# Attention into a soft mixture of experts: one pool of named places, six streams of row sums, every step's position from a table

## The chip, the cores and the metric

The kernel runs on one core of one Trainium2 chip. The metric is the device time in microseconds of one execution of the whole program; the time of the kernel before is the median of three runs. The profile is one execution taken by the hardware profiler; all times in it count from its first instruction.

## The reference, cut to what matters

Inputs are q, k, v of shape (8, 8, 576, 64), phi (512, 32), w1 (8, 512, 1024) and w2 (8, 1024, 512).

```python
q_rot, k_rot = (rotate(q), rotate(k))              # rotary positions
scores = 1/sqrt(64) * np.matmul(q_rot, k_rot.transpose(0, 1, 3, 2))
attn = np.exp(scores - np.max(scores, axis=-1, keepdims=True))
attn = attn / (np.sum(attn, axis=-1, keepdims=True) + 1e-09)
x = np.matmul(attn, v)                             # regrouped to (4608, 512)
logits = x @ phi                                   # 32 slots
d = softmax(logits, axis=0); c = softmax(logits, axis=1)
slot_input = d.T @ x                               # 4 slots for each of 8 experts
slot_out[e] = np.maximum(slot_input[e] @ w1[e], 0.0) @ w2[e]
out = c @ slot_out
```

## The kernel before, in words

**Pairs.** Two heads make a pair, so there are 32 pairs, four to a batch of the input. For each pair the queries and keys come in (`fetch`, L135), GpSimd multiplies them by cosine and sine in eight pieces (`spin`, L140), VectorE adds the halves (`join`, L144), ScalarE casts to fp16 (`high`, L149) and VectorE subtracts the cast to get the low part (`low`, L153).

**Maxima.** In nine groups of four matmuls (`m_unit`, L173, and `m_rem`, L181) TensorE makes the scores by rows into PSUM and VectorE reduces each group to row maxima (L175, L183). The maxima are turned, scaled and sent as two rows to the partitions of `peak` (`m_turn`, `m_half`, `m_rows`).

**Scores and values.** In nine blocks of keys (`t_unit`, L220) TensorE makes the transposed scores with the maximum subtracted, in 16 matmuls; ScalarE takes the exponential into `a_t` (two blocks to a tile) or `a_rem` (the ninth, L221). `av` (L236) multiplies a block with the values, four fp32 matmuls, each two records in the trace. Maxima, scores, sums, turned tiles and logits all take turns in one PSUM pool of three tiles (`bank2`).

**Row sums.** VectorE adds the four two-block tiles into `c_t` (`add`, L253 twice with 1152 columns, L255 once with 576). `total` (L265) sums the partitions of four streams (both halves of `c_t`, `a_rem`, the first half of the last `a_t`) by matmuls with a matrix of ones and zeros, eight per pair, 32 output partitions each, side by side. `total_out` (L270) copies the result out, `send` (L276) moves it by four small DMAs onto 96 partitions, `recip` (L282, L283) adds the four streams and takes the reciprocal, `spread` and `widen` bring it back over all partitions through DRAM, and `norm` on GpSimd multiplies the output of the attention.

**Slots.** From the normalised output come logits (`logits`, L348), the turned rows `xn` (`natural`, L334), and after every fourth pair the slots' running sums (`slot_tasks`, L395, L398) and the softmax over slots. After the last pair come two expert layers (`ffn1`, L773; `ffn2_steps`, L797), the collecting of slot outputs (`gather`, L810) and the output (`combine`, L825), 18 stores of 512 KB.

**Expert weights.** 64 tiles of 512 KB come through SyncE's queue (`load_w`, L482). 25 have places of their own. The others wait until a pool of the attention is closed: `release_io` after the last `low`, `release_stk` and `release_att` behind the last pair, and at last the place of `xn`.

**What sets the order.** All five engines run in the order in which the program is written. The table `WHEN` gives each step one position in a beat of four units per pair, the same for every pair; the opening and the closing are written by hand. In the opening, VectorE copies four small squares of the identity (`fold`, L630) before the first maxima.

Of the kernel before, what the change touches and what calls it, by code (L numbers as in the profile page):

```python
# [17 lines left out]
NP = H // 2  # L18
# [10 lines left out]
N_W = 25  # L29
N_WA = 5  # L30
N_WB = 2
N_WE = 3
N_WL = 2
N_X = 4
N_CS = 1
N_CE = 2
C_POOL = 4
LATE = (0, 2)
N_LEAD = 7
# [4 lines left out]
N_CST = 4 - N_CE  # L44
RC = 12
PIECE = 4
WHEN = {
    "load0": -15.9, "load1": -14.496, "spin0": -13.466, "spin1": -12.4, "join": -9.9, "high0": -9.4817, "high1":
    -9.0595, "low": -8.0, "m01": -6.5262, "m10": -5.894, "m00": -5.0601, "m11": -4.7, "load_v": -3.85, "m20": -3.771,
    "m21": -3.317, "m30": -2.9, "m31": -2.7, "m_rem": -2.6642, "m_min": -2.49, "m_turn": -1.744, "m_half": -1.667,  # L50
# [4 lines left out]
    "o_out": 4.52, "add3": 4.6009, "total": 5.54, "total_out": 5.55, "send": 5.56, "sums_turn": 6.0, "sums_wide": 6.3,  # L55
    "norm_wide": 6.4, "logits_late": 7.0, "logits_sum_late": 7.05, "recip": 7.294, "natural_late": 7.3, "spread": 7.31,
    "natural_out_late": 7.35, "widen": 7.3768, "norm": 8.706, "logits": 10.54, "logits_sum": 10.579, "stats": 11.3708,
    "natural": 11.52, "natural_out": 11.536,
}
QL, QH, KH, KL = range(4)  # L60
# [3 lines left out]
def attn_softmoe(ctx, tc, qk, v, phi, w1, w2, cs, ident, sel, seg, out):  # L64
# [5 lines left out]
    wp = ctx.enter_context(tc.tile_pool(name="wp", bufs=N_W))  # L70
    left = ctx.enter_context(ExitStack())
    xp = left.enter_context(tc.tile_pool(name="xp", bufs=1))
    vals = ctx.enter_context(ExitStack())
    late = vals.enter_context(tc.tile_pool(name="late", bufs=2))
    trans = ctx.enter_context(ExitStack())
    att = trans.enter_context(tc.tile_pool(name="att", bufs=1))
    early = ctx.enter_context(ExitStack())
    stk = early.enter_context(tc.tile_pool(name="stk", bufs=4))
    right = ctx.enter_context(ExitStack())
    io = right.enter_context(tc.tile_pool(name="io", bufs=1, side="right"))  # L80
# [5 lines left out]
        engines={mybir.EngineType.PE, mybir.EngineType.Activation, mybir.EngineType.DVE}))  # L86
    steady = ctx.enter_context(ExitStack())
    steady.enter_context(tc.manual_schedule(engines={mybir.EngineType.SP, mybir.EngineType.Pool}))

    rows = (slice(0, 64), slice(64, P))  # L90
    cs_sb = io.tile([P, 2, S], F32, name="cs_sb")
# [3 lines left out]
    bits = const.tile([P, 5], F32, name="bits")  # L95
    ones, warm, tiny, fold = bits[:, 0:1], bits[:, 1:2], bits[:, 2:3], bits[:, 3:5]
# [27 lines left out]
    c_tiles = []  # L124
# [4 lines left out]
    def load(p):  # L129
        loaded[p] = io.tile([P, 2, 2, S], F32, name="x_in", bufs=2)  # L130
# [78 lines left out]
    def t_unit(p, b):  # L209
        if b == KB - 1:  # L210
            rems[p] = att.tile([P, S], F32, name="a_rem")
        elif b % 2 == 0:
            ats[p, b // 2] = att.tile([P, 2, S], F32, name="a_t", bufs=4)
# [28 lines left out]
    def o_out(p):  # L242
        xts[p] = late.tile([P, S], F32, name="xt")
        nc.scalar.copy(out=xts[p].rearrange("p (n x) -> p n x", n=2), in_=os_.pop(p)[:, :, 0:HC])  # L244
# [13 lines left out]
    rcs = [const.tile([96, 4, RC], F32, name=f"rc{i}") for i in range(2)]  # L258

    def total(p):  # L260
        c, r, a = cts.pop(p), rems[p], ats[p, 3]
        sg[p] = s = bank2()
        for n in range(2):
            for i, m in enumerate((c[:, 0], c[:, 1], r, a[:, 0])):
                nc.tensor.matmul(s[32 * i:32 * i + 32, n, 0:HC], lhsT=pick[:, n:n + NS], rhs=m[:, half[n]],  # L265
                                 start=True, stop=True, tile_position=(0, 32 * i))

    def total_out(p):
        s, s4 = sg[p], late.tile([P, S], F32, name="s4", bufs=1)
        nc.scalar.activation(out=s4.rearrange("p (n x) -> p n x", n=2), in_=s[:, :, 0:HC], func=AF.Identity, bias=tiny)  # L270
# [15 lines left out]
    def spread(p, eng):  # L286
        rr = sg.pop(p)
        rd = dram.tile([2, S], F32, name="r_row")
        eng.dma_start(out=rd.rearrange("h (r x) -> (h r) x", x=RC), in_=rr)
        sg[p] = rd  # L290

    def widen(p, eng):
        rd = sg.pop(p)
        rbs[p] = rb = late.tile([P, S], F32, name="rb", bufs=1)
        for h in range(2):
            eng.dma_start(out=rb[rows[h]], in_=rd[h:h + 1].broadcast_to([64, S]))
# [4 lines left out]
    def sums_turn(p):  # L301
        s4 = sg.pop(p)
        t = bank2()
        for j in range(5):
            w = P if j < 4 else 64
            nc.tensor.matmul(t[0:w, 0, 2 * j:2 * j + 2], lhsT=s4[:, P * j:P * j + w], rhs=fold, start=True, stop=True)
        rn = small.tile([P, RC], F32, name="rr", bufs=2)
        nc.vector.reciprocal(out=rn[:, 0:8], in_=t[:, 0, 0:8])
        nc.vector.reciprocal(out=rn[0:64, 8:10], in_=t[0:64, 0, 8:10])
        sg[p] = rn  # L310

    def sums_wide(p):
        rn = sg.pop(p)
        sg[p] = t = bank2()
        for j in range(5):
            w = P if j < 4 else 64
            for h in range(2):
                nc.tensor.matmul(t[rows[h], j // 4, P * (j % 4):P * (j % 4) + w],
                                 lhsT=rn[0:w, 2 * j + h:2 * j + h + 1].broadcast_to([w, 64]), rhs=id_sb[0:w, 0:w],
                                 start=True, stop=True)  # L320

    def norm_wide(p):
        t, xt = sg.pop(p), xts[p]
        nc.vector.tensor_tensor(out=xt[:, 0:512], in0=t[:, 0], in1=xt[:, 0:512], op=ALU.mult)
# [609 lines left out]
```

## Time and profile before

| what | value |
|---|---|
| time, three runs | 613.80, 610.75, 618.16 us; median 613.8 |
| span of the profiled execution | 611.8 us, from the first to the last instruction; no time of its own is given beside it |
| mean granted TensorE clock | 0.959 of full speed |
| DMA | 111.63 MB in 71734 packets |
| weight loads | 63 of 512 KB under one name, one under another |

In the page, busy is the union of an engine's instructions; matmul ends are modelled. The chain of waits follows the last instruction back to what released it. Idle time of an engine costs nothing where another engine sets the end.

### The profile page before, as it was taken

How to read it: one execution, taken by the hardware profiler on the slowest of the kernel's cores; microseconds unless marked ns; L12 is line 12 of the kernel's file. 1: busy time of each engine (PE TensorE's matmuls, PEld its weight loads, DVE VectorE, ACT ScalarE, POOL GpSimd, SP SyncE). 2: the span in 40 equal slices, each digit the busy share in tenths (PEclk: the TensorE clock that was granted, in tenths of full speed). 3: DMA queues.
4: the chain of work that ended last, by engine and by line, in shares of the span. 5: the costliest groups of instructions: out<-in, count | busy, mean ns of one | idle time of the engine just before them, and what ended most of it. 6: DMA issues, size and time to landing. Idle time of an engine off the chain costs nothing.

```text
span 611.8 us, 23277 instructions
## 1 busy us (share of the span) xinstructions
PE 532.9 (87%) x10064; PEld 352.1 (58%) x10064; DVE 497.0 (81%) x729; ACT 326.9 (53%) x647; POOL 315.1 (52%) x308
## 2 busy tenths in 40 slices
PE   3668999998999899989999899898898999799981
PEld 2346666656765566666656565666566666443551
DVE  6879899999998999999998999999899874322341
ACT  2145656665665565656656566565465655324441
POOL 2668498655676566647763857658654000100000
PEclk9679999999999999999999999999899999859996
DMA  7153555555555555555555555455542246649999
GB/s 260 60 195 119 175 174 173 174 174 173 174 173 174 174 174 174 173 175 174 174 173 175 173 174 174 174 174 174 171 141 62 64 130 206 206 142 350 349 376 298
DMA packets 71734, 111.63 MB, mean 182 GB/s; under 512 B 20176, under 2 KB 47568, under 8 KB 71632
## 3 DMA queue, kind: packets, MB, share of 16 engines
q1 hardware_dynamic: 71618, 110.15, 54.5%
q8 instruction: 79, 1.29, 0.9%
q14 instruction: 23, 0.19, 0.1%
q10 hardware_dynamic: 14, 0.00, 0.0%
HBM read 99.93 MB, written 9.58 MB: 179 GB/s over the span
## 4 chain that ended last, share of the span: by engine, by line
PE 35%; DVE 26%; DMA 20%; ACT 6%; SPq 5%; issue 5%; POOL 1%; DVEq 0%; ACTq 0%
PE s_ps L220 8%; PE o_ps L236 8%; DVE nm L175 7%; DMA rc<-s 7%; DMA w_exp<-in_w 6%; DVE c_t L253 6%; DVE hl L153 5%; SPq L276 4%; ACT a_t L221 3%; PE s_ps L265 3%; DMA x_in<-in_qk 3%; PE s_ps L773 3%; DMA v_in<-in_v 2%; DVE c_t L255 2%; PE s_ps L173 2%
## 5 line engine op out<-in xcount | busy, mean ns | idle before, releaser
L140 POOL TENSOR_TENSOR x_in<-x_in,cs_sb 128x288 f32<-128x288 f32 x248 | 264.9, 1101 | 63.0 <-DMA x_in<-in_qk 38.1
L221 ACT ACTIVATE a_t<-s_ps 128x576 f32<-128x576 f32 x256 | 158.9, 649 | 97.8 <-PE s_ps L220 95.9
L175 DVE TENSOR_REDUCE nm<-s_ps 128x2 f32<-128x576 f32 x256 | 187.1, 743 | 15.1 <-PE s_ps L173 14.9
L236 PE MATMUL o_ps<-a_t,v_in 64*64 64x288 f32 x2048 | 172.4, 413 | 1.0 <-ACT xt L244 0.3
L220 PE MATMUL s_ps<-hl 64*64 64x288 f16 x3456 | 155.5, 286 | 16.4 <-DVE nm L175 15.9
L220 PEld LDWEIGHTS <-hl 64*64 64x64 f16 x3456 | 104.4, 107 | 59.9 <-issue 43.8
L299 POOL TENSOR_TENSOR xt<-xt,rb 128x576 f32<-128x576 f32 x30 | 42.8, 1425 | 141.0 <-DMA rb<-r_row 104.1
L173 PE MATMUL s_ps<-hl 64*64 64x288 f16 x1024 | 82.1, 298 | 26.0 <-DVE nm L175 20.5
L220 PE MATMUL s_ps<-peak,lift 64*64 64x288 f16 x1152 | 89.1, 284 | 0.0
L236 PEld LDWEIGHTS o_ps<-a_t,v_in 64*64 64x64 f32 x2048 | 72.9, 133 | 21.0 <-issue 7.3
L173 PEld LDWEIGHTS <-hl 64*64 64x64 f16 x1024 | 45.0, 107 | 49.1 <-issue 37.7
L149 ACT CAST hl<-x_in 128x576 f16<-128x576 f32 (+1 forms) x66 | 40.1, 650 | 33.1 <-DVE x_in L144 30.3
L270 ACT ACTIVATE s<-s_ps,bits 128x576 f32<-128x576 f32 x32 | 23.7, 740 | 58.0 <-PE s_ps L265 26.3
L144 DVE TENSOR_TENSOR x_in<-x_in 128x1152 f32<-128x1152 f32 (+2 forms) x36 | 53.4, 1483 | 0.5 <-POOL x_in L140 0.4
L253 DVE TENSOR_TENSOR c_t<-c_t,a_t 128x1152 f32<-128x1152 f32 x32 | 51.6, 1611 | 0.0
L153 DVE TENSOR_TENSOR hl<-x_in,hl 128x1152 f16<-128x1152 f32 x32 | 49.5, 1546 | 1.8 <-ACT hl L149 1.8
L253 DVE TENSOR_TENSOR c_t<-a_t 128x1152 f32<-128x1152 f32 x32 | 50.6, 1582 | 0.0
L220 PEld LDWEIGHTS <-lift 64*64 64x64 f16 x1152 | 38.1, 108 | 0.6
L265 PE MATMUL s_ps<-c_t,pick 128*32 128x288 f32 x256 | 37.1, 411 | 0.0
L265 PE MATMUL s_ps<-a_rem,pick 128*32 128x288 f32 x128 | 36.9, 411 | 0.0
L265 PE MATMUL s_ps<-a_t,pick 128*32 128x288 f32 x128 | 36.9, 411 | 0.0
L221 ACT ACTIVATE a_rem<-s_ps 128x576 f32<-128x576 f32 x32 | 20.8, 651 | 17.0 <-PE s_ps L220 17.0
(183 smaller groups left out, 597.6 us busy)
## 6 DMA issues: line engine op xcount, KB each, us to landing
x_in<-in_qk SPq DMA_DIRECT2D x62, 576.0 KB
w_exp<-in_w SPq DMA_DIRECT2D x63, 512.0 KB
v_in<-in_v SPq DMA_DIRECT2D x32, 576.0 KB
rb<-r_row SPq DMA_DIRECT2D x60, 144.0 KB
out<-w_exp SPq DMA_DIRECT2D x16, 512.0 KB
rc<-s SPq DMA_DIRECT2D x120, 4.5 KB
x_in<-in_qk SPq DMA_DIRECT2D x4, 288.0 KB
out<-w_exp SPq DMA_DIRECT2D x4, 256.0 KB
```

Source lines behind the costliest of these rows:

```text
L140: eng.tensor_tensor(out=x[:, :, c], in0=x[:, :, c], in1=cs_sb[:, :, c], op=ALU.mult)
L144: nc.vector.tensor_tensor(out=x[:, t, 0, c], in0=x[:, t, 0, c], in1=x[:, t, 1, c], op=ALU.add)
L149: nc.scalar.copy(out=halves[p][:, 1 + t, c], in_=loaded[p][:, t, 0, c])
L153: nc.vector.tensor_tensor(out=hl[:, 0:4:3], in0=x[:, :, 0], in1=hl[:, 1:3], op=ALU.subtract)
L173: nc.tensor.matmul(s[rows[c], h, 0:HC], lhsT=hl[rows[h], QH, at:at + D], rhs=hl[rows[h], KH, half[n]], start=True, stop=True)
L175: nc.vector.tensor_reduce(out=nms[p][:, n, j:8:4], in_=s[:, :, 0:HC], axis=AX.X, op=ALU.max, negate=True)
L220: nc.tensor.matmul(s[rows[h ^ n], n, 0:HC], lhsT=lhs, rhs=rhs, start=(i == 0), stop=(i == 3))
L221: nc.scalar.activation(out=weights_of(p, b).rearrange("p (n x) -> p n x", n=2), in_=s[:, :, 0:HC], func=AF.Exp, scale=SCALE)
L236: nc.tensor.matmul(o[rows[h], n, 0:HC], lhsT=vt[r, b, n], rhs=a[r, half[n]], start=(b == 0), stop=(b == KB - 1))
L253: nc.vector.tensor_tensor(out=c, in0=c if j > 1 else ats[p, 0], in1=a, op=ALU.add)
L265: nc.tensor.matmul(s[32 * i:32 * i + 32, n, 0:HC], lhsT=pick[:, n:n + NS], rhs=m[:, half[n]], start=True, stop=True, tile_position=(0, 32 ...
L299: eng.tensor_tensor(out=xts[p], in0=xts[p], in1=rbs.pop(p), op=ALU.mult)
```

## The change

One pool (`big`) holds all large tiles under fixed names, each a place: two for the inputs (`x0`, `x1`), four for the fp16 parts (`hl0` to `hl3`), two for values, four for the exponentials (`a0` to `a3`), and so on. It stays open to the end. A weight tile is loaded into a place right behind the place's last reader: `fill` is a step like the others, 0.8 units behind the last `low`, `t8` or `av8` that reads there. Weights of their own have 28 places (`w`), which also hold the later tiles of the closing part; results go out from nine of the attention's places.

The row sums have six streams, in two sets of three that accumulate in PSUM: `c` (now the sum of the first two tiles, its first half with the first half of the third added), the second half of the third, both halves of the fourth, and the ninth block. That is two additions on VectorE and twelve matmuls. The result has 288 columns, and two sends go out in place of four.

Every step has its own position for each of the four pairs of a batch, and one of its own for each of the first four pairs; the batch's steps (`ENDS`), the opening's single steps (`ONCE`) and the last pair but one (`LAST`) are in tables too. GpSimd makes `fold` in one instruction, in place of VectorE's four copies.

```diff
-N_W = 25
+N_W = 28
+LAG = 0.8
+FILL = (6, 8, 5)
+PLACES = ("x0", "x1", "cs", "hl0", "hl1", "hl2", "v0", "hl3", "a0")
-    "o_out": 4.52, "add3": 4.6009, "total": 5.54, "total_out": 5.55, "send": 5.56, "sums_turn": 6.0, "sums_wide": 6.3,
+    4.6881, 4.3287, 3.6811), "o_out": (4.8784, 4.7532, 4.6296, 4.2983), "total": (5.7529, 5.5594, 5.1412, 4.9378),
+    "total_out": (5.8475, 5.7089, 5.282, 4.971), "send": (6.4739, 6.3131, 6.1856, 5.6953), "recip": (6.8303, 6.8467,
+    7.2922, 6.5543), "spread": (7.8252, 7.2981, 7.5691, 7.5261), "widen": (8.6569, 8.8329, 7.6411, 8.2716), "norm":
...
     def add(p, j):
         if j == 1:
-            cts[p] = att.tile([P, 2, S], F32, name="c_t")
-        c, a = cts[p], ats[p, j]
-        if j < 3:
-            nc.vector.tensor_tensor(out=c, in0=c if j > 1 else ats[p, 0], in1=a, op=ALU.add)
+            cts[p] = big.tile([P, 2, S], F32, name="c")
+            nc.vector.tensor_tensor(out=cts[p], in0=ats[p, 0], in1=ats[p, 1], op=ALU.add)
         else:
-            nc.vector.tensor_tensor(out=c[:, 1], in0=c[:, 1], in1=a[:, 1], op=ALU.add)
+            c = cts[p][:, 0]
+            nc.vector.tensor_tensor(out=c, in0=c, in1=ats[p, 2][:, 0], op=ALU.add)
...
     def total(p):
-        c, r, a = cts.pop(p), rems[p], ats[p, 3]
+        c, a2, a3 = cts.pop(p), ats[p, 2], ats[p, 3]
+        streams = ((c[:, 0], c[:, 1], a2[:, 1]), (a3[:, 0], a3[:, 1], rems[p]))
         sg[p] = s = bank2()
-        for n in range(2):
-            for i, m in enumerate((c[:, 0], c[:, 1], r, a[:, 0])):
-                nc.tensor.matmul(s[32 * i:32 * i + 32, n, 0:HC], lhsT=pick[:, n:n + NS], rhs=m[:, half[n]],
-                                 start=True, stop=True, tile_position=(0, 32 * i))
+        for i in range(3):
+            for k in range(2):
+                for n in range(2):
+                    g = 32 * (n + 2 * k)
+                    nc.tensor.matmul(s[g:g + 32, 0, 0:HC], lhsT=pick[:, 16 * n:16 * n + 32], rhs=streams[k][i][:, half[n]],
+                                     start=(i == 0), stop=(i == 2), tile_position=(0, g))
...
     def send(p, eng):
         s4, rc = sg.pop(p), rcs[p % 2]
-        for i in range(4):
-            eng.dma_start(out=rc[:, i, :], in_=s4[32 * i:32 * i + 2])
+        for k in range(2):
+            eng.dma_start(out=rc[:, k, :], in_=s4[64 * k:64 * k + 64:16])
...
+    def turn_w():
+        load_w(big.tile([P, 1024], F32, name="w", bufs=N_W))
+
+    def fill(tag):
+        n = 2 if tag[0] == "x" else 1
+        t = big.tile([P, n, 1024], F32, name=tag)
+        for i in range(n):
+            load_w(t[:, i])
...
-    nc.vector.memset(fold, 0.0)
-    for i in range(0, P, 32):
-        nc.vector.tensor_copy(out=fold[i:i + 2], in_=id_sb[i:i + 2, i:i + 2])
+        nc.gpsimd.tensor_tensor(out=fold, in0=id_sb[:, 0:64:16], in1=id_sb[:, 64:128:16], op=ALU.add)
...
+    frees = {("low", 30): ("x0",), ("low", 31): ("x1", "cs"), ("t8", 28): ("hl0",), ("t8", 29): ("hl1",),
+             ("t8", 30): ("hl2",), ("av8", 30): ("v0",)}
+    tasks.extend([(at + LAG, "fill", tag) for at, name, p in tasks for tag in frees.get((name, p), ())])
+
+    for at, name, p in sorted(tasks):
+        if name == "fill":
+            fill(p)
+        else:
+            do(name, p)
...
+    for tag in ("hl3", "a0", "a1", "a2", "a3", "c"):
+        fill(tag)
...
+    xw = big.tile([P, 2560], F32, name="xn")
+    for i in range(2):
+        load_w(xw[:, 1024 * i:1024 * i + 1024])
...
+        for _ in range(FILL[2 * grp + f - 1]):
+            turn_w()
```

What the tables do to the instructions is seen in the order on the engines. First VectorE in the opening, before and then after: L140 and L172 are the multiplications, L175 and L207 the maxima, `bits` holds `fold`.

```order
L144 TENSOR_TENSOR x_in<-x_in 128x288
L153 TENSOR_TENSOR hl<-x_in,hl 128x2x576
L628 MEMSET bits 128x2
L630 COPY bits<-id_sb 2x2 x4
L175 TENSOR_REDUCE nm_192<-s_ps 128x2 x6
L144 TENSOR_TENSOR x_in<-x_in 128x576
```

```order
L176 TENSOR_TENSOR x_106<-x_106 128x288
L185 TENSOR_TENSOR hl_117<-x_106,hl_117 128x2x576
L207 TENSOR_REDUCE nm_154<-s_ps 128x2 x6
L176 TENSOR_TENSOR x_113<-x_113 128x576
L207 TENSOR_REDUCE nm_154<-s_ps 128x2
```

The copies of the identity no longer stand between the first `low` and the first maxima.

Next TensorE in a pair of the steady stretch, before and then after: L236 and L268 are products with the values (x12 is three blocks, x4 one), L173 and L205 maxima, L220 scores.

```order
L220 LDWEIGHTS lift
L220 MATMUL s_ps<-peak_102,lift 64x288
L236 MATMUL o_ps<-a_t,v_in 64x288 x12
L173 LDWEIGHTS hl
L173 MATMUL s_ps<-hl 64x288
```

```order
L268 MATMUL o_ps<-a_2602,v_2302 64x288 x4
L205 LDWEIGHTS hl_2591
L205 MATMUL s_ps<-hl_2591 64x288
L205 LDWEIGHTS hl_2591
L205 MATMUL s_ps<-hl_2591 64x288
L205 LDWEIGHTS hl_2591
L205 MATMUL s_ps<-hl_2591 64x288
L205 LDWEIGHTS hl_2591
L205 MATMUL s_ps<-hl_2591 64x288
L268 MATMUL o_ps<-a_2602,v_2302 64x288 x4
```

Three blocks that stood together are now taken one by one, with a group of maxima between. In this order a pair has up to nine products that stand alone; the last pairs of the kernel before have five such and two of two blocks.

Last SyncE at the end, before and then after: L482 and L512 are weight loads, L296 and L330 `widen`, L515 and L648 the table `seg`, L829 and L795 results; the tile's name is the place.

```order
L296 DMA rb<-r_row 64x576 x2
L482 DMA w_exp<-in_w 128x2x512 x3
L482 DMA w_exp<-in_w 128x4x256
L482 DMA wk<-in_w 128x2x512
L482 DMA w_exp<-in_w 128x4x256 x3
L515 DMA seg_in<-in_seg 128x320
L482 DMA w_exp<-in_w 128x4x256 x2
L482 DMA w_exp_11365<-in_w 128x4x256
L482 DMA w_exp_11367<-in_w 128x4x256
L482 DMA w_exp<-in_w 128x4x256 x24
L829 DMA out<-w_exp_11653 128x4x256
```

```order
L330 DMA rb<-r_row 64x2x288 x2
L512 DMA v_10986<-in_w 128x4x256
L512 DMA w<-in_w 128x4x256
L648 DMA rb<-in_seg 128x320
L512 DMA hl_11209<-in_w 128x4x256
L512 DMA a_11211<-in_w 128x4x256
L512 DMA a_11213<-in_w 128x4x256
L512 DMA a_11215<-in_w 128x4x256
L512 DMA a_11217<-in_w 128x4x256
L512 DMA c<-in_w 128x4x256
L512 DMA xn<-in_w 128x4x256 x2
L512 DMA w<-in_w 128x4x256 x19
```

Before, 26 loads stand behind the release of `xn`, the last three rows of loads above; after, 21.

## Rows read from the trace of the kernel before

**Rows 1.** The page, busy time: us, share of the span, instructions.
```profile
PE 532.9 (87%) x10064; PEld 352.1 (58%) x10064; DVE 497.0 (81%) x729; ACT 326.9 (53%) x647; POOL 315.1 (52%) x308
```

**Rows 2.** Chain of waits: start us, us, what.
```profile
54.36 1.21 PE s_ps L265 x16
...
301.67 2.03 DMA rc<-s
...
484.26 1.15 PE s_ps L265 x16
...
488.73 1.46 PE o_ps L236 x24
490.18 0.12 PE s_ps L173 x4
...
498.74 1.00 PE s_ps L398 x8
499.74 0.97 PE s_ps L265 x16
...
506.76 0.65 PE o_ps L236 x8
...
509.97 0.65 ACT xt L244
...
512.35 1.11 PE s_ps L265 x16
```

**Rows 3.** Busy time by stretch: the 28 steady pairs, one pair without maxima.
```profile
54.40:484.30 429.90, 394.03 (x8223) 269.80 (x8227) 405.86 (x570) 258.92 (x506) 273.27 (x249) 1.00 0.50 165
499.70:512.35 12.65, 12.33 (x264) 7.95 (x256) 6.62 (x14) 7.96 (x17) 0.00 (x0) 1.00 0.34 110
```

**Rows 4.** Who waited for whom: us in total, times, longest us.
```profile
PE s_ps L173 <- DVE nm L175: 20.5, 24, 3.9
...
PE s_ps L220 <- DVE nm L175: 15.9, 34, 1.8
...
DVE rr L282 <- DMA rc<-s: 7.5, 13, 1.4
```

**Rows 5.** Busy time by stretch, closing part; last two columns DMA share, GB/s.
```profile
500.00:512.40 12.40, 12.08 (x256) 7.87 (x252) 6.43 (x14) 8.01 (x17) 0.00 (x0) 1.00 0.33 107
...
525.40:542.50 17.10, 13.38 (x116) 8.88 (x112) 6.33 (x21) 5.86 (x16) 3.53 (x8) 0.67 0.70 222
...
549.00:563.00 14.00, 13.98 (x125) 5.45 (x122) 4.42 (x10) 5.35 (x13) 0.87 (x1) 1.00 1.08 351
```

**Rows 6.** Timeline of SyncE's queue at the end: start us, us, issues.
```profile
526.23 51.97 SPq L482 DMA_DIRECT2D w_exp<-in_w  x28
...
592.35 11.74 SPq L829 DMA_DIRECT2D out<-w_exp  x8
604.19 2.71 SPq L832 DMA_DIRECT2D out<-w_exp  x2
```

**Rows 7.** Chain of waits, closing part.
```profile
576.82 8.55 DMA w_exp<-in_w
...
589.62 0.68 PE s_ps L810 x4
```

**Rows 8.** Groups by line, 97.9 to 344: busy us, mean ns, idle before.
```profile
L253 DVE TENSOR_TENSOR c_t<-c_t,a_t 128x1152 f32<-128x1152 f32 x16 | 27.0, 1686 | 0.0
```

**Rows 9.** The same operation in the view of its tile: ns min/median/max.
```profile
L253 DVE TENSOR_TENSOR c_t<-c_t,a_t x32: 1344/1352/1959, 48.6 to 520.3; 128x1152 f32<-128x1152 f32 x32
```

**Rows 10.** Timeline of the opening, VectorE and TensorE.
```profile
13.11 2.86 DVE L630 COPY bits<-id_sb 2x2 f32<-2x2 f32 x4
16.00 4.08 DVE L175 TENSOR_REDUCE nm<-s_ps 128x2 f32<-128x576 f32 x6
...
16.81 0.45 PE L173 MATMUL s_ps<-hl 64*64 64x288 f16 x4 [3.91 <-DVE nm L175]
```

More of the change, by code (lines that the diff above doesn't have):

```diff
@@ L69, in attn_softmoe @@
     small = ctx.enter_context(tc.tile_pool(name="small", bufs=3))
[L70 to L80, printed above, removed]
+    big = ctx.enter_context(tc.tile_pool(name="big", bufs=1))
     dram = ctx.enter_context(tc.tile_pool(name="dram", bufs=3, space=bass.MemoryType.DRAM))
@@ L293, in widen @@
         rd = sg.pop(p)
-        rbs[p] = rb = late.tile([P, S], F32, name="rb", bufs=1)
+        rbs[p] = rb = big.tile([P, S], F32, name="rb")
         for h in range(2):
-            eng.dma_start(out=rb[rows[h]], in_=rd[h:h + 1].broadcast_to([64, S]))
+            eng.dma_start(out=rb[rows[h]].rearrange("p (n x) -> p n x", n=2),
+                          in_=rd[:, h].unsqueeze(0).broadcast_to([64, 2, HC]))
     def norm(p, eng):
@@ L314, in sums_wide @@
         sg[p] = t = bank2()
[L315 to L320, printed above, removed]
+        for n in range(2):
+            for j in range(3):
+                w = P if j < 2 else 32
+                for h in range(2):
+                    at = 4 * j + 2 * n + h
+                    nc.tensor.matmul(t[rows[h], n, P * j:P * j + w],
+                                     lhsT=rn[0:w, at:at + 1].broadcast_to([w, 64]), rhs=id_sb[0:w, 0:w],
+                                     start=True, stop=True)
     def norm_wide(p):
-        t, xt = sg.pop(p), xts[p]
-        nc.vector.tensor_tensor(out=xt[:, 0:512], in0=t[:, 0], in1=xt[:, 0:512], op=ALU.mult)
-        nc.vector.tensor_tensor(out=xt[:, 512:S], in0=t[:, 1, 0:64], in1=xt[:, 512:S], op=ALU.mult)
+        t, xt = sg.pop(p), xts[p].rearrange("p (n x) -> p n x", n=2)
+        nc.vector.tensor_tensor(out=xt, in0=t[:, :, 0:HC], in1=xt, op=ALU.mult)
     def natural(p):
@@ L463, in attn_softmoe, with load_w @@
     w_tiles = {}
-    extra = []
-    later = []
-    swap = list(range(4, 5 + N_CST))
-    order = [n for n in range(8 * E) if n not in swap]
-    order[N_W:N_W] = swap[:-1]
-    order.insert(N_W + N_CST + N_WA, swap[-1])
-    def load_w(pool, bufs, tag="w_exp"):
-        n = order[len(w_tiles)]
+    def load_w(place):
+        n = len(w_tiles)
         layer, rest = divmod(n, 4 * E)
@@ new lines, in attn_softmoe, with end, run, rest @@
+    nc.scalar.activation(out=warm, in_=ones, func=AF.Exp)
+    ends = {}
+    def end(name):
+        def run(p):
+            if p not in ends:
+                ends[p] = {"stat": stat_tasks(p // NP), "comb": c_soft_tasks(p // NP)}
+            if name == "slot" and name not in ends[p]:
+                ends[p]["slot"] = slot_tasks(p // NP)
+            next(ends[p][name], None)
+        return run
+    def rest(begin, task):
+        return lambda p: task(p) if p else begin()
+    def begin_load():
+        load(0)
+        for t, cc in ((1, 0), (1, 1), (0, 0), (0, 1)):
+            c = half[cc]
+            if t:
+                nc.sync.dma_start(out=cs_sb[:, :, c], in_=cs[:, :, c])
+            nc.sync.dma_start(out=loaded[0][:, t, :, c], in_=qk[0, t][:, :, c])
@@ new lines, in begin_spin, with heat, tables, folds @@
+    def begin_spin(t):
+        for c in half:
+            spin(0, t, nc.vector, (c,))
+            join(0, t, c)
+            high(0, t, c)
+    def heat(n):
+        o = bank2()
+        for i in range(n):
+            nc.tensor.matmul(o[:, 0, 0:HC], lhsT=lift, rhs=halves[0][:, KH, 0:HC], start=True, stop=True)
+    def tables():
+        nc.sync.dma_start(out=phi_sb, in_=phi.rearrange("(c p) n -> p c n", p=P))
+        nc.sync.dma_start(out=sel_sb, in_=sel)
+    def folds():
+        nc.gpsimd.tensor_tensor(out=fold, in0=id_sb[:, 0:64:16], in1=id_sb[:, 64:128:16], op=ALU.add)
@@ L593, in do @@
     def do(name, p):
-        if (name, p) not in done and 0 <= p < NPAIR:
+        if (name, p) not in done:
             done.add((name, p))
             plan[name](p)
-    beat = sorted((when % 4, int(when // 4), name) for name, when in WHEN.items())
-    load(0)
-    for t, cc in ((1, 0), (1, 1), (0, 0), (0, 1)):
-        c = half[cc]
-        if t:
-            nc.sync.dma_start(out=cs_sb[:, :, c], in_=cs[:, :, c])
-        nc.sync.dma_start(out=loaded[0][:, t, :, c], in_=qk[0, t][:, :, c])
@@ L606, in attn_softmoe @@
-    do("load0", 1)
-    do("load1", 1)
-    nc.sync.dma_start(out=id_sb, in_=ident)
-    do("load_v", 0)
-    for t in (1, 0):
-        for c in half:
-            spin(0, t, nc.vector, (c,))
-            join(0, t, c)
-            high(0, t, c)
-    o = bank2()
-    def heat(n):
-        for i in range(n):
-            nc.tensor.matmul(o[:, 0, 0:HC], lhsT=lift, rhs=halves[0][:, KH, 0:HC], start=True, stop=True)
-    heat(N_WARM)
-    low(0)
-    done.update((n, 0) for n in ("spin0", "spin1", "join", "high0", "high1", "low", "load0", "load1"))
@@ L662, in attn_softmoe @@
-    for p in range(NPAIR):
-        for _, back, name in beat:
-            do(name, p - back)
-        if not extra and ("low", NPAIR - 1) in done:
-            release_io()
-    p = NPAIR - 1
-    while later:
-        trickle(p)
-    while pending:
-        step(p)
-    release_stk()
-    for name in ("add1", "add2", "av4", "av5", "add3", "av6", "av7", "av8", "o_out", "total", "total_out"):
-        do(name, p)
-    steady.close()
-    release_att()
+    tasks = [(at, name, 0) for name, at in ONCE.items()]
```

333 lines of the change are left out of this document (134 added, 199 removed), and 33 rows, old and new, of tables (FIRST, WHEN).

## The prediction

> **What bounds the kernel now.** I first read the page's busy shares [rows 1]: TensorE 87%, VectorE 81%, the others near half. That is an average over an opening, a steady attention and a closing part, so I cut the span. The chain of waits shows where the matmuls of the row sums (line 265, once per pair) start: from 54.36 to 484.26 there are 28 pairs, 15.35 us each [rows 2]. In that stretch VectorE is busy 405.86 of 429.90 us, 94%, or 14.5 us per pair, and TensorE 394.03, 92% [rows 3]. Two engines near the top: which one sets the pace? The view of who waited for whom says that TensorE's named waits are on VectorE's maxima (20.5 and 15.9 us), since a maximum is read straight from PSUM and the pool of score tiles has three places [rows 4]. So VectorE is the bound of the 28 pairs.
>
> How close TensorE is behind it, the last pairs tell. Pairs 30 and 31 have no maxima left beside them: from 499.74 to 512.35 a pair takes 12.61 us [rows 2], TensorE is busy 12.33 of 12.65 us there and VectorE only 6.62 [rows 3]. A pair without maxima therefore costs TensorE about 12.6 us when nothing of VectorE holds it.
>
> The closing part is another regime. From 549 on the DMA engines move 351 GB/s with a share over 1, while at 500 to 512 they move 107 and at 525 to 542 222 [rows 5]. SyncE's row of 28 weight loads, issued over 51.97 us from 526.23, runs into the row of results [rows 6]: the tail waits for transfers that could not start because their places were still in use. The chain of waits shows 8.55 us on such a load [rows 7].
>
> **The sums, on VectorE.** Before, a pair has two additions of 1152 columns and one of 576; after, one of each. So one of 1152 goes: its mean is 1686 ns in the steady stretch [rows 8], and over all pairs it lies between 1344 and 1959 [rows 9]. VectorE's own need falls from 14.5 to 12.8 us per pair by the mean, to 13.2 by the shortest. Why one shape takes 1344 or 1959 the rows do not say; if it is a wait for another engine, a part of it may pass to the next addition, and so I keep both ends. Neither moves the forecast, which TensorE sets; both stand in rival (a).
>
> **The sums, on TensorE.** The matmuls of the sums go from 8 to 12 per pair, in the trace from 16 records to 24. Sixteen take 0.97 to 1.21 us on the chain [rows 2], so eight more cost 0.5 to 0.6. Nothing hides them: they stand in the engine's own order. I take 0.5. The evacuation on ScalarE halves to 288 columns and the sends from four to two; ScalarE and SyncE's queue are not on the path in the steady stretch, and I cost both at nothing.
>
> **The new positions.** The order shows most products with the values alone between scores and maxima where before up to three stood together. Three in a row cost 1.46 us, 0.49 each, one alone 0.65 [rows 2]. The measured pair of 12.61 us has five alone, the new order up to nine: four more at 0.16 is 0.6 us at most, and nothing at best, if a wait was what made the lone one long.
>
> So TensorE's need per pair after: 12.6, plus nine groups of maxima at 0.12 [rows 2], 1.1, plus a batch's slot matmuls, 1.00 and some transposes in every fourth pair [rows 2], 0.3, plus 0.5 for the sums: 14.5 us. It is now above VectorE's 12.8 to 13.2, so TensorE becomes the bound and VectorE's relief is only partly collected: 15.35 - 14.5 = 0.85 us, times 28 pairs, 23.9 us. The bounds: 13.8 if the waits of 0.7 us that the 12.61 may still hold go as well (the pair had 0.3 us of idle TensorE and one evacuation of ScalarE on its chain), an estimate from the rows; 15.1 if all nine lone products cost their full 0.16. I take 14.5, because it rests on a pair that was measured with TensorE almost never idle.
>
> In the last three pairs the maxima thin out and end, and TensorE sets the pace already before: the added matmuls cost 3 x 0.5 = 1.5 us there.
>
> **The opening.** Four copies of two rows each (line 630, 2.86 us) stand on VectorE at 13.11, right before the first maxima at 16.00, and TensorE waits 3.91 us for those [rows 10]. They go to GpSimd, much later, as one instruction. The whole opening is VectorE's, so 2.9 us come off; with the shorter additions of the first pair 4.0. Bounds: 2, if the late loads of the first pairs take some of it back, and 6, if the warm-up matmuls that now stand between the first maxima keep the clock up.
>
> **The places.** Of the 64 weight loads, 26 stand behind the release of the slot inputs before (28 in SyncE's last row of them, less the first two); now 21. Five loads of 0.52 MB less at 351 GB/s [rows 5] are 7.5 us less for the queue. But the path of the matmuls is not much shorter: the last gather is at 589.62 [rows 7], its waits for loads just before are a few us of the 8.55, and behind it nine results of 0.52 MB need 1.5 us each in the queue, from 592.35 to about 607 [rows 6], whichever way. What can go is the waits for loads and the queue's backlog. Bounds 1.5 and 7.5; I take 5.3, nearer to the queue's number, because the queue is full to the end. The early fills stand on SyncE ahead of sends and value loads, but in a stretch where the queue is at a third of its rate; cost nothing, and 5 us if that cover fails (a rival).
>
> **The sum**, made against the profiled span of 611.8 us: 611.8 - 23.9 - 4.0 - 5.3 + 1.5 = 580.1. The median of the runs is 613.8, 2.0 above the span; what lies around it stays. Forecast 582 us.
>
> **Rivals.**
> (a) TensorE has room, and VectorE stays the bound at its lower need: 12.8 to 13.2 plus today's 0.85 of idle time, 13.7 to 14.05. In the middle that is 28 x 1.5 = 42 us instead of 23.9: 564 us. For it: its named waits are 36 us only. Against it: the measured 12.61 us with VectorE half idle. The Trainium skill, page "Perfetto Trace Analysis", section "Identifying the Most-Contended Engine", judges TensorE's headroom by the busy share of weight loads, not of matmuls; here that is 58% [rows 1], so by that rule added matmuls would be nearly free. The pairs without maxima speak against the rule here: weight loads busy 7.95 of 12.65 us, 63% [rows 3], and yet the pace is TensorE's. Chance 0.14.
> (b) The pool of three score tiles keeps TensorE waiting as it does now, and lone products cost in full: 15.1 us, 7 us from the pairs, 599 us. For it: VectorE's maxima must still come within three tiles. Chance 0.17.
> (c) The early fills do not do what they say: SyncE, in order, waits for a place to come free and holds back the value loads and maxima rows of the last four pairs. The tail's 5.3 us are gone and some 5 are added: 592 us. Chance 0.12.
> (d) Slower: the reciprocals now stand closer behind their sums in three pairs of four (1.1, 1.3 and 1.6 units of the table, 1.75 before). A send needs the sums' matmuls (1.5 us), an evacuation, the issue and 2.03 us in flight [rows 2]; VectorE waits 7.5 us for it in 13 pairs now [rows 4]. VectorE has 1.3 us of room under 14.5. If it stands 3 us idle in each pair, a pair takes 13.2 + 3.0 = 16.2 us, 24 us more over 28 pairs, less 7.8 from both ends: 628 + 2 = 630. It is slower than before from a wait of 2.4 us per pair on. Chance 0.04.
> The forecast itself, 14.2 to 14.8 us per pair and 574 to 591 us, has 0.53.
>
> **Range and chances.** 566 to 601 takes in the forecast, (b), (c) and the bounds 13.9 and 15.1 of a pair; it leaves out (d) and most of (a). About 1% is what a measurement of this kernel can tell from no change: 607.7 and 619.9 us. Faster by more 0.91, within it 0.05 (the upper end of (b) with nothing gained at the ends), slower 0.04.
>
> **What would show it.** The row sums' matmuls 14.5 us apart in the steady stretch; VectorE near 13 us of that, TensorE above 95% and its waits on maxima under half of today's; 24 records of the sums in 1.5 us; the first maxima about 3 us earlier; 21 loads behind the release and no wait of a matmul for a load near the end. I am wrong if the steady pairs come under 13.9 (TensorE had room) or over 15.1 (its waits were not VectorE's load), if VectorE waits for sends, or if SyncE's last pairs show waits for places ahead of value loads.

## The result, and the profile after

The changed kernel takes 585.0 us (median of four runs, 581.0 to 590.0), the kernel before 612.3 (its three runs and one more). The ratio is 0.954, 95% interval 0.946 to 0.961; it leaves out the slow execution of 590.0. Forecast were 582 us and 566 to 601. The profiled execution of it took 582.4, its span 580.6.

The page of the changed kernel, busy time (us, share of the span, instructions), against [rows 1]:

```profile
PE 522.4 (90%) x10320; PEld 353.8 (61%) x10320; DVE 439.4 (76%) x690; ACT 322.2 (55%) x647; POOL 303.4 (52%) x309
```

VectorE has 57.6 us less to do. To see where the time went, the span is cut where the matmuls of the sums (now line 299) and of the experts start. The timeline of TensorE has these starts of the 29th and the last pair's sums and of the first expert matmul:

```profile
452.27 0.44 PE L299 MATMUL s_ps<-c,pick 128*32 128x288 f32 x2
...
497.45 0.44 PE L299 MATMUL s_ps<-c,pick 128*32 128x288 f32 x2
...
516.00 1.94 PE L741 MATMUL s_ps<-w,slot_t 128*32 128x512 f32 x8 [0.47 <-DVE slot_t L731]
```

The first sums are on the chain of waits, with their 24 records:

```profile
41.40 1.66 PE s_ps L299 x24
```

| stretch | before, us | after, us | change | forecast |
|---|---|---|---|---|
| start to first sums | 54.4 [rows 2] | 41.4 | -13.0 | -4.0 |
| 28 pairs | 429.9 [rows 2] | 410.9 | -19.0 | -23.9 |
| next three pairs | 41.1 [rows 2, 5] | 45.2 | +4.0 | +1.5 |
| last sums to first expert matmul | 17.1 [rows 5] | 18.6 | +1.5 | 0 |
| experts to the end | 69.3 [rows 5] | 64.6 | -4.7 | -5.3 |
| sum | | | -31.2 | -31.7 |

The sum came out to half a microsecond; only the last term did so nearly, and the opening and the pairs missed by 9.0 and 4.9 us in opposite directions. A steady pair takes 410.87 / 28 = 14.67 us, and the busy times of 24 of these pairs (from the fifth sums; PE, PEld, DVE, ACT, POOL, then granted clock, DMA share, GB/s) tell who is at the limit:

```profile
97.95:452.27 354.32, 338.54 (x7274) 235.29 (x7273) 309.51 (x475) 219.81 (x444) 222.38 (x214) 1.00 0.55 178
```

TensorE 14.11 of 14.76 us, 96%; VectorE 12.90. Six of the executions profiled below hold the same instructions in these pairs (this one, the split moved, the fills late, the copies, the warm-up, both edits). They took 14.56 to 14.81 us a pair, so a difference under 0.25 us between two profiles tells little.

Who waited for whom, over the span, against [rows 4]:

```profile
DVE nm L207 <- PE s_ps L205: 34.5, 61, 1.8
...
PE s_ps L384 <- POOL xt L334: 13.8, 8, 3.8
...
PE s_ps L205 <- DVE nm L207: 4.6, 6, 1.6
...
PE s_ps L252 <- DVE nm L207: 3.2, 5, 1.2
```

VectorE now waits for TensorE's scores; TensorE's waits for maxima are 4.6 and 3.2 us (20.5 and 15.9 in [rows 4]). New is that TensorE stands idle ahead of the logits (line 384), whose input GpSimd's product (line 334) has not finished.

Two new waits lie at the end. The timeline of SyncE's queue and then GpSimd's, at the 28th pair:

```profile
446.22 0.38 SPq L512 DMA_DIRECT2D cs<-in_w  x1
446.74 0.89 SPq L512 DMA_DIRECT2D x<-in_w  x2
447.72 2.55 SPq L512 DMA_DIRECT2D hl<-in_w  x1
450.38 1.31 SPq L330 DMA_DIRECT2D rb<-r_row  x2
...
458.74 1.40 POOL L334 TENSOR_TENSOR xt<-xt,rb 128x576 f32<-128x576 f32 x1 [16.09 <-DMA rb<-r_row]
```

The early fills stand in the queue ahead of the widened reciprocals (rb): 8.4 us from issue to GpSimd's product. The issue itself is late too. From 444 to 453 SyncE's queue has this wait ahead of a weight load, for matmuls that must be through before the place may be filled:

```profile
SPq L512 <- PE s_ps L205: 2.2, 1, 2.2
```

TensorE waits 3.82 us for the product from 456.4 on, and from 460 to 464 us it works at a mean granted clock of 0.60. In the closing part VectorE (first row) waits for the slot denominators and TensorE (second) for VectorE:

```profile
512.00 0.42 DVE L715 TENSOR_SCALAR zw<-e_sel,zs 128x32 f32<-128x32 f32 x1 [4.15 <-POOL zs L711]
...
512.48 0.63 PE L717 MATMUL t_ps<-zw,bits 128*128 128x32 f32 x2 [3.16 <-DVE zw L715]
```

On GpSimd `zs` stands behind the split of the second quarter (line 467, at 509.95), which waits for ScalarE. In the kernel before, GpSimd and SyncE were bound to the written order only up to the last pair; its trace has `zs` at 534.77 us, ahead of this split at 540.35.

### The profile page after: what moved, and what is told of

Read it like the earlier page. It is cut to its first block, busy times and chain, and to the rows that moved or that the text cites. A ratio compares the mean times of both kernels' runs of the same rounds, so it can differ in the third digit from the quotient of the medians.

```text
span 580.6 us, 23543 instructions
## 1 busy us (share of the span) xinstructions
PE 522.4 (90%) x10320; PEld 353.8 (61%) x10320; DVE 439.4 (76%) x690; ACT 322.2 (55%) x647; POOL 303.4 (52%) x309
## 4 chain that ended last, share of the span: by engine, by line
PE 57%; DMA 15%; DVE 13%; ACT 4%; issue 4%; POOL 3%; SPq 2%; ACTq 0%; POOLq 0%; DVEq 0%
PE o_ps L268 15%; PE s_ps L252 14%; DMA rb<-r_row 7%; PE s_ps L299 6%; PE s_ps L205 4%; DVE nm L207 4%; DMA x<-in_qk 4%; DVE hl L185 3%; PE s_ps L741 3%; POOL xt L334 3%; PE s_ps L370 2%; DMA rc<-s 2%; PE s_ps L384 2%; PE t_ps L791 2%; PE o_ps L765 1%
## 5 line engine op out<-in xcount | busy, mean ns | idle before, releaser
L172 POOL TENSOR_TENSOR x<-x,cs 128x288 f32<-128x288 f32 x248 | 249.3, 1039 | 80.5 <-DMA x<-in_qk 73.7
L207 DVE TENSOR_REDUCE nm<-s_ps 128x2 f32<-128x576 f32 x256 | 185.5, 750 | 36.1 <-PE s_ps L205 34.5
L253 ACT ACTIVATE a<-s_ps 128x576 f32<-128x576 f32 x256 | 159.7, 653 | 83.4 <-PE s_ps L252 79.7
L268 PE MATMUL o_ps<-a,v 64*64 64x288 f32 x2048 | 171.8, 408 | 0.6
L205 PE MATMUL s_ps<-hl 64*64 64x288 f16 x1024 | 81.5, 292 | 5.5 <-DVE nm L207 4.6
L268 PEld LDWEIGHTS o_ps<-a,v 64*64 64x64 f32 x2048 | 70.7, 133 | 12.8 <-issue 3.9
L205 PEld LDWEIGHTS <-hl 64*64 64x64 f16 x1024 | 38.6, 105 | 37.7 <-issue 23.0
L299 PE MATMUL s_ps<-a,pick 128*32 128x288 f32 x384 | 52.2, 409 | 0.0
L181 ACT CAST hl<-x 128x576 f16<-128x576 f32 (+1 forms) x66 | 42.3, 659 | 16.6 <-DVE x L176 16.4
L185 DVE TENSOR_TENSOR hl<-x,hl 128x1152 f16<-128x1152 f32 x32 | 50.2, 1569 | 0.5 <-ACT hl L181 0.5
L283 DVE TENSOR_TENSOR c<-a,a 128x1152 f32<-128x1152 f32 x32 | 49.3, 1542 | 0.0
L176 DVE TENSOR_TENSOR x<-x 128x1152 f32<-128x1152 f32 (+2 forms) x36 | 45.2, 1256 | 0.2
L299 PE MATMUL s_ps<-c,pick 128*32 128x288 f32 x256 | 37.1, 411 | 0.2
L276 ACT COPY xt<-o_ps 128x576 f32<-128x576 f32 x32 | 20.5, 639 | 12.4 <-PE o_ps L268 6.6
```

What stands on the lines that cost most here:

```text
L172: eng.tensor_tensor(out=x[:, :, c], in0=x[:, :, c], in1=cs_sb[:, :, c], op=ALU.mult)
L176: nc.vector.tensor_tensor(out=x[:, t, 0, c], in0=x[:, t, 0, c], in1=x[:, t, 1, c], op=ALU.add)
L185: nc.vector.tensor_tensor(out=hl[:, 0:4:3], in0=x[:, :, 0], in1=hl[:, 1:3], op=ALU.subtract)
L205: nc.tensor.matmul(s[rows[c], h, 0:HC], lhsT=hl[rows[h], QH, at:at + D], rhs=hl[rows[h], KH, half[n]], start=True, stop=True)
L207: nc.vector.tensor_reduce(out=nms[p][:, n, j:8:4], in_=s[:, :, 0:HC], axis=AX.X, op=ALU.max, negate=True)
L253: nc.scalar.activation(out=weights_of(p, b).rearrange("p (n x) -> p n x", n=2), in_=s[:, :, 0:HC], func=AF.Exp, scale=SCALE)
```

## Experiments

Theory: the gain in the pairs is the sums', TensorE is the bound now, and the new waits cost about 5 + 2 + 10 us. Rivals: VectorE still sets the pace; the positions carry the gain; the waits only move. All edits are to the changed kernel, except that the six sums alone are put into the kernel before; the last runs build on each other.

**The split moved.**
```diff
     c_tr(0)
-    c_split(1)
     list(c_evac(0))
...
     nc.vector.tensor_scalar_mul(out=zw, in0=e, scalar1=zs)
+    c_split(1)
```


> The changed kernel with one step of the closing part moved: the split of the second quarter of the combine weights (a copy on ScalarE, a subtraction on GpSimd) stands behind the slot denominators on GpSimd instead of ahead of them. Theory: in the changed kernel GpSimd's subtraction waits for that ScalarE copy, the denominators (zs) wait behind it, VectorE waits 4.15 us for zs and TensorE 3.16 us for VectorE, right on the chain to the first expert matmul; so 2.5 to 3.5 us come off the 585. Rival: the stretch is held by the weight loads or by the state update on VectorE as well, and less than 1 us comes off.

582.0 us, ratio 0.946 (0.939 to 0.952). The interval overlaps the changed kernel's, so the time alone does not show a gain. The trace shows the piece: `zw` starts at once, and last sums to expert matmul take 16.7 us for 18.6, 1.9 us less where 2.5 to 3.5 was expected. That is the least of it: the five executions with the split behind take 15.1 to 17.2 us here, the seven with it ahead 18.6 to 21.3. The unchanged opening took 3.2 us longer in this execution (first sums at 44.60); of that below.

**More work on TensorE, on VectorE, and VectorE's in pieces.** The first runs the matmuls of the sums twice, the second the large addition; the third, run later, adds three maxima of the accumulator with itself.
```diff
-        for i in range(3):
+        for i in (0, 1, 2, 0, 1, 2):
```
```diff
-            nc.vector.tensor_tensor(out=cts[p], in0=ats[p, 0], in1=ats[p, 1], op=ALU.add)
+            for _ in range(2):
+                nc.vector.tensor_tensor(out=cts[p], in0=ats[p, 0], in1=ats[p, 1], op=ALU.add)
```
```diff
+    def piece():
+        t = acc[:, 0:384]
+        nc.vector.tensor_tensor(out=t, in0=t, in1=t, op=ALU.max)
...
-            plan[f"m{j}{n}"] = lambda p, j=j, n=n: m_unit(p, j, n)
+            plan[f"m{j}{n}"] = lambda p, j=j, n=n: (m_unit(p, j, n), n == 0 and 0 < j and piece())
```


> The changed kernel with the twelve matmuls of the row sums made twice in each pair (the second time over the first, same result): 24 records more on TensorE, nothing more on any other engine. Theory (TensorE sets the pace of the steady pairs, busy 14.04 of 14.67 us): a pair gets longer by the 1.46 to 1.66 us that 24 records take, less the 0.6 us of idle time at most; over 32 pairs 30 to 53 us, 615 to 638 us. Rival (VectorE or a latency still sets the pace, TensorE has room): under 15 us, 585 to 600.

> The changed kernel with the addition of 1152 columns made twice in each pair (same result): 1.54 us more on VectorE per pair, nothing more on TensorE, so VectorE is as loaded as in the kernel before (14.4 us). Theory (TensorE sets the pace, VectorE has 1.8 us of room in 14.67): the pair gets longer by 0.2 to 0.7 us, since maxima come later behind the longer row of additions; 590 to 608 us. Rival (VectorE sets the pace): 1.54 us x 32 = 49 us, 634.

> The changed kernel with more work on VectorE in three pieces: a maximum of 384 columns of the slot accumulator with itself, which changes nothing, behind three of the nine maxima of each pair, about 0.55 us each and 1.6 us per pair, as much as the doubled addition. Theory one (VectorE's room is real, and the doubled addition cost 1.1 us per pair because the maxima stood behind one long row): the pieces cost under 0.6 us per pair, 590 to 603 us. Theory two (with three score tiles TensorE and VectorE go in turns, so work on either makes the pair longer in whatever form): 0.9 us or more per pair, 613 and above.

612.4, 616.8 and 609.4 us (ratios 0.997, 1.000, 0.992). Busy time of the same 24 pairs, columns as above; matmuls twice:

```profile
102.00:476.58 374.58, 370.17 (x7850) 253.91 (x7849) 308.06 (x475) 218.55 (x444) 215.32 (x214) 1.00 0.54 169
```
addition twice:
```profile
105.74:486.92 381.18, 342.15 (x7275) 235.21 (x7273) 348.61 (x499) 221.23 (x444) 245.20 (x214) 0.99 0.53 166
```
in pieces:
```profile
106.74:478.03 371.29, 342.69 (x7274) 235.67 (x7272) 350.10 (x547) 220.94 (x444) 236.53 (x215) 1.00 0.54 170
```

With the matmuls twice, TensorE is busy 99% of a pair of 15.61 us: 0.85 us more for 1.32 of added busy time, since the idle time falls from 0.66 to 0.18 us. TensorE's own need is thus some 14.1 us, and it is the nearer bound. The total missed the theory's range by 3 us but is far from the rival's. The doubled addition was a plain miss: 15.88 us per pair, 1.12 more, where 0.2 to 0.7 was expected. VectorE needs 14.53 there and TensorE 14.26: neither is full. In pieces (0.69 us each in the mean, not 0.55) about the same VectorE load, 14.59, makes 15.47, 0.71 more, between the two theories: about a third of the cost was the one long row, the rest is not, as far as one profile of each tells. At that load the pair is as in the kernel before, 14.5 in 15.35 [rows 3]: VectorE as the bound leaves 0.9 us idle. Taken off 14.7, its load could grow to 13.8 before it decides. By this estimate its room is 0.9 us, not 14.7 - 12.9 = 1.8; no run was made at that load.

**The sums alone, in the kernel before** (short; the sends, the reciprocals and the closing sums follow the new layout, old pools and positions stay).
```diff
-            for i, m in enumerate((c[:, 0], c[:, 1], r, a[:, 0])):
+        streams = ((c[:, 0], c[:, 1], a2[:, 1]), (a3[:, 0], a3[:, 1], rems[p]))
```


> The kernel before with the six streams of sums alone: one addition of 1152 columns less, twelve matmuls for eight, half the evacuation, two sends for four; old positions, old pools. Theory (the pairs gain by the sums, the positions only serve them): a pair goes from 15.35 to 14.5 to 14.9 us, 13 to 24 us come off the 612, 588 to 599. Rival (without the new positions VectorE's relief is not collected, since maxima and additions still come in the order that made TensorE wait): less than 6 us, 606 to 612.

600.3 us, ratio 0.976 (0.970 to 0.982): one microsecond above the theory's range, six below the rival's. Over the 24 pairs one takes (473.65 - 112.16) / 24 = 15.06 us, against (484.19 - 112.84) / 24 = 15.47 before and 14.76 with everything. So the sums give 0.41 us a pair, about half of the gain. The rest, 0.25 to 0.5 us by the scatter of the six executions, came with the positions and pools, which were not tried without the sums. It is not idle time that goes: with the sums alone TensorE is busy 14.45 of 15.06 us, with everything 14.11 of 14.76.

```profile
112.16:473.65 361.49, 346.79 (x7277) 236.78 (x7273) 323.55 (x475) 220.94 (x444) 236.15 (x214) 1.00 0.51 168
```

**The fills late.**
```diff
-    frees = {("low", 30): ("x0",), ("low", 31): ("x1", "cs"), ("t8", 28): ("hl0",), ("t8", 29): ("hl1",),
-             ("t8", 30): ("hl2",), ("av8", 30): ("v0",)}
-    tasks.extend([(at + LAG, "fill", tag) for at, name, p in tasks for tag in frees.get((name, p), ())])
...
-    for tag in ("hl3", "a0", "a1", "a2", "a3", "c"):
+    for tag in ("x0", "x1", "cs", "hl0", "hl1", "hl2", "v0", "hl3", "a0", "a1", "a2", "a3", "c"):
```


> The changed kernel with the nine early fills (weight loads into the places of the attention, each behind its last reader) moved behind the last pair, where six more stand already. Theory: nine loads of 0.52 MB are 13.4 us at 351 GB/s that have to go through the queue between the last pairs and the results; the expert matmuls then wait for loads and results come out later, 3 to 8 us more, 588 to 593. Rival (the queue has the room near the end, the matmuls are the path anyway): within 1.5 us, 584 to 587.

580.4 us, ratio 0.944 (0.934 to 0.953): both sides missed, it is not slower at all. The experts take 64.4 us as before the edit (64.6), and the three pairs 39.7 for 45.2 (39.7 in all four runs with late fills, 43.0 to 47.5 in all eight with early ones). The timelines of SyncE and GpSimd at the 28th pair, where the rows above had the fills:

```profile
448.81 0.39 SPq L323 DMA_DIRECT2D r_row<-rr  x1
450.44 1.75 SPq L330 DMA_DIRECT2D rb<-r_row  x2
...
454.97 1.41 POOL L334 TENSOR_TENSOR xt<-xt,rb 128x576 f32<-128x576 f32 x1 [8.86 <-DVE nm L207]
```

4.5 us from issue to product, and there GpSimd no longer waits for the transfer last. The issue of rb comes 1.6 us behind that of r_row, where it was 4.6 with the fills between. Early fills gain nothing and cost 5.5 us.

**Copies and warm-up back.** Four copies of two rows on VectorE ahead of the second maxima, into a tile not read; the sixteen warm-up matmuls behind the first pair's transpose (of both, the tables alone are shown).
```diff
-    "ids": -3.1435,
+    "ids": -3.75, "copies": -3.31,
```
```diff
-"heat1": -2.4787
+"heat1": -1.17
```


> The changed kernel with the memset and the four copies of two rows put back on VectorE ahead of the second maxima, into a tile that nobody reads, and the load of the identity far enough ahead of them. Theory (the opening is VectorE's): 2.9 us of copies come on top at the first maxima, and TensorE stands idle longer there; 2.5 to 6 us more, 587 to 591. Rival (a later wait, for the loads of the third pair or for the first maxima rows, takes it up): under 1 us.

> The changed kernel with the second group of sixteen warm-up matmuls moved back behind the first pair's maxima and their transpose. Theory: there VectorE waits for the next pair's scores until the warm-up is through (2.8 us of waiting in the kernel before), and the first pair's maxima run with TensorE near idle; 2 to 5 us more, 587 to 590. Rival (the warm-up costs the same at either place): under 1 us.

590.0 us (0.960) and 585.3 (0.952): by the time, the theory for the copies and the rival for the warm-up. Start of the first and the fifth sums, and the mean granted clock from 16 to 20 us:

| execution | first sums, us | fifth sums, us | clock |
|---|---|---|---|
| changed kernel | 41.40 | 97.95 | 1.00 |
| split moved | 44.60 | 101.27 | 0.50 |
| fills late | 44.45 | 101.00 | 0.65 |
| copies back | 48.33 | 104.19 | 0.50 |
| warm-up back | 44.71 | 103.27 | 0.50 |

The second and third rows have the changed kernel's opening, untouched. Against them the copies cost 3.7 to 3.9 us at the first sums and 2.9 at the fifth. The warm-up's place costs 0.1 to 0.3 at the first sums. Its 2.0 at the fifth come from one long pair (16.7 us) ahead of them, such as the changed kernel has later; neither the first sums nor the time shows a gain from that place.

**Logits later.** With the split behind as well; the transposes to rows go 0.5 later (cut).
```diff
-"logits": (10.4353, 9.7107, 10.2396, 10.2058)
+"logits": (11.0353, 10.3107, 10.8396, 10.8058)
```


> The changed kernel with the split of the second quarter behind the slot denominators, and besides with the logits of each pair 0.6 of the table's units later (2.2 us) and the transposes to rows 0.5 later. Theory (TensorE stands idle 0.6 us per pair, 0.4 of it before logits that come ahead of GpSimd's product): the waits for that product fall from 9.9 us in the steady pairs to under 3, a pair takes 14.1 to 14.4 us, 6 to 11 us come off, 571 to 578. Rival (the idle time only moves, to the transposes or to the maxima): 579 to 584, as with the split alone.

586.2 us, ratio 0.953: the rival, or worse. The waits for GpSimd's product fell from 9.9 to 5.1 us in the steady pairs, and yet a pair took 14.94:

```profile
100.17:458.78 358.61, 345.18 (x7274) 236.12 (x7272) 310.36 (x475) 218.54 (x444) 219.02 (x214) 1.00 0.56 176
```

TensorE's idle time did fall, from 0.66 to 0.56 us a pair, but its busy time rose from 14.11 to 14.38 with the same matmuls at the same clock; the six executions have 14.05 to 14.18. So taking the consumer later gained nothing, though not by moving the idle time as the rival has it. What makes the matmuls take longer is open.

**Both edits, and loads behind.** The first run holds late fills and the late split; the second also puts three loads of every four pairs behind the widened reciprocals (in the table, of `load0`, `load_v` and `weights`).
```diff
-    "load0": (-16.4019,
+    "load0": (-16.3,
...
-    -3.5908, -3.5209)
+    -3.5908, -3.3)
...
-    24.7539, 1.8856
+    24.9, 1.8856
```


> The changed kernel with both single edits: the nine early fills behind the last pair, and the split of the second quarter behind the slot denominators. Theory: the early fills stand in the DMA queue ahead of the widened reciprocals of the last pairs and cost 5 us there, the split costs 2 to 3 us in the closing part, and the two are apart in time; 575 to 579 us. Rival (the late fills push the closing part, which the split then cannot shorten): 580 to 583, as either alone.

> As the run with both edits, and besides three loads of 0.5 MB (the first half of x of every fourth pair, the values of every fourth, a weight tile of every fourth) issued right behind the widened reciprocals of a pair instead of right ahead of them. Theory (in the steady pairs, as in the last ones, the widened reciprocals wait in the queue behind such a load, GpSimd's product comes late, and TensorE stands idle ahead of the logits, 9.9 us): those waits fall to under 4 us and 4 to 8 us come off against the run with both edits, 569 to 573. Rival (the idle time moves, as it did when the logits were put later): within 2 us of that run.

573.3 us (0.933, 0.928 to 0.937) and 564.7 (0.920, 0.916 to 0.925), so the edits do not get in each other's way (11.7 us under the changed kernel, 3.0 and 4.6 alone), and the loads give 8.7 us more. Who waited for whom in the 24 pairs, without and then with the loads behind:

```profile
PE s_ps L384 <- POOL xt L334: 9.7, 7, 2.1
```
```profile
PE s_ps L384 <- POOL xt L334: 2.9, 3, 1.9
```

A pair goes from 14.73 to 14.39 us, below all six executions with the loads ahead; TensorE's busy time is 14.03. Bringing the producer earlier did what moving the consumer later did not. This is the fastest version, 20 us under the changed kernel.

**Warm-up between the maxima,** on top of that.
```diff
-        o = bank2()
+        o = ps_o.tile([P, 2, 512], F32, name="o_ps")
...
+    "heat2": -3.25, "heat3": -1.7,
...
-        "heat1": lambda p: heat(16),
+        "heat1": lambda p: heat(12),
+        "heat2": lambda p: heat(12),
+        "heat3": lambda p: heat(14),
```


> As the last run (both edits and the three loads behind), and besides the warm-up matmuls of the opening written to the place of the value products instead of a score tile, with 12 more between the first pair's first maxima and 14 ahead of its transpose, where TensorE stands idle 1.6 and 3.2 us. Theory (the first sums came at 41.4 us where the granted clock was 1.00 up to 24 us, at 43.7 to 44.6 where it fell to half from about 13 to 16 us on, with the same program): the clock stays at 1.00 through the first maxima, the first sums come at 41 to 42 us in every execution, 561 to 563 us. Rival (the opening is VectorE's and the clock only goes along, or the added matmuls come in the way): 564 to 567.

568.2 us (0.926, 0.923 to 0.930): 3.5 more. The first sums did come at 41.9 (43.7 without), but the pairs took 14.45 us, and last sums to end 3.0 longer, with the clock low over a longer part of the first expert matmuls. Why is open; one profiled execution of each does not tell it from chance.

## Why the prediction was right, and where it was not

- **The bound moves to TensorE**: it is busy 96% of a pair, and 99% with the matmuls twice. Pairs of 14.67 us lie within 14.2 to 14.8. The term was mis-sized by 4.9 us: it held no wait ahead of the logits, which is 9.9 us in the 24 pairs. With the loads behind the widened reciprocals 6.8 of 9.7 us of this wait go, and 28 pairs take 14.32 us each. So the mechanism was right, TensorE's own need lies a little under 14.5, and the wait was left out. The eight added records cost what was said: 24 in 1.66 us here, 16 in 1.21 at the same place [rows 2].
- **Rival (a)** fell: added matmuls were not near free. The Trainium skill's rule ("Perfetto Trace Analysis", "Identifying the Most-Contended Engine"), which judges TensorE's headroom by MFU (the share of the peak arithmetic rate) and the busy share of its weight loads, would by the latter find room at 61%; the runs disagree, with 0.85 us per pair for 24 matmuls. The rival's floor for VectorE, need plus 0.85, held with the work in pieces: 15.47 at a need of 14.59. With the addition twice the pair lay higher, 15.88 at 14.53.
- **Rival (b)**, 15.1 us, fell: maxima cost TensorE 4.6 and 3.2 us. Its idea that the two go in turns is right beyond the forecast: more work on VectorE cost 0.7 to 1.1 us per pair where I saw 1.3 of room. The price of lone products was a misreading. In a steady pair after:

```profile
203.37 0.65 PE L268 MATMUL o_ps<-a,v 64*64 64x288 f32 x8
203.85 0.29 PE L205 MATMUL s_ps<-hl 64*64 64x288 f16 x4
```

The lone product lasts 0.65 us, but the next group starts 0.48 us after its start: its tail is overlapped. It costs a third of three in a row (0.49), and the 0.16 for each of four more comes to nothing.

- **Rival (c)** was half right, and here a step failed: "in a stretch where the queue is at a third of its rate; cost nothing". The fills cost 5.5 us, and the sign named for it showed: SyncE stood 2.2 us for a place ahead of rb and of a value load. At the 28th pair rb went out 3.0 us later behind r_row, and then took 3.8 longer to its reader behind loads of 0.5 MB. Without the fills the last three pairs take 39.7 us, about 1.5 less than before, where I had added 1.5. The tail's gain, which this rival gave up, stayed.
- **The places**: 21 loads behind the release, 64.6 us instead of 69.3, and the wait of 8.55 us [rows 7] is gone. The size was right (-4.7 for -5.3; the other runs with these places take 63.3 to 66.0 us). It owes nothing to the early fills; fifteen loads issued after the last pair do as well.
- **The opening** failed in size: -13.0 for -4.0, out of its bounds. The first maxima start at 13.07 us for 16.00 [rows 10], the 2.9 forecast. With the copies back the first sums come 3.7 to 3.9 us later, and about 3 us of the 13.0 are this execution's fast opening, as against other executions of the same opening. The warm-up's place shows 0.3 us at most. About 6 us stay open: the positions, with the third pair's x loaded from 26.61 on for 31.40, were not tried by themselves.
- **Closing part**: the split on GpSimd was not in the account; 1.9 us at least.
- **Rival (d)** did not come: VectorE's waits for sends were 4.0 us over the span (7.5 in [rows 4]).

The mechanism in the pairs was right, but the total was right by luck, through offset: the opening gave 9.0 us more than I had, and the pairs 4.9, the last three 2.5, the closing part 1.5 and the end 0.6 less.

## What to carry to other kernels

When a bound moves, ask what the new bound will wait for besides the old one: here small transfers at the end of a long chain, for which bulk loads are better issued behind than ahead. Taking a wait away at its producer paid 8.7 us, moving its consumer nothing. Room on the second engine was not the difference of the busy times; as an estimate, take off the idle time that it had when it was the bound itself. Price a group of matmuls by the time to the next group's start, not by its length. Before reading a small difference between two profiles, look how far unchanged stretches differ.

## What was not expected of the hardware

- The same opening differs by some 3 us between executions. With the clock near 1.00 up to 24 us the first sums came at 41.4 (changed kernel, matmuls twice) and 41.5 us (both edits); where it fell to half between 12 and 20 us they came at 43.7 to 44.6. In the profile of the kernel before it was 0.50 from 16 to 24 us as well. Two executions, 16 to 20 us, changed kernel and then fills late:

```profile
16.00:20.00 4.00, 2.59 (x28) 1.73 (x26) 3.88 (x5) 0.00 (x0) 4.00 (x6) 1.00 0.86 254
```
```profile
16.00:20.00 4.00, 3.48 (x19) 2.29 (x19) 3.12 (x5) 0.00 (x0) 4.00 (x6) 0.65 0.86 283
```

- A transfer of 0.3 MB took 8.4 us from issue to the start of its reader behind four loads, 4.5 without. The Trainium skill ("DMA: Bandwidth & Descriptors", "Queues, rings and completion order") says that each DMA engine takes a queue's descriptors in the order of the ring; the rows agree.
- More work on VectorE goes with slower GpSimd operations: GpSimd's busy time for the same 214 of them in the 24 pairs is 222 us, and 245 with the addition twice.
